# A SwiGLU kernel's prologue: x in two loads, first weight pieces in slices, transposed x evicted by slice

## The chip, the cores and the metric

One core of one Trainium2 chip. The metric is the device time of one execution in microseconds (us), 126.12 us for the kernel before (median of the first 4 runs). The profile's span, from the first to the last instruction, is 1.7 us shorter than the time of the same run (124.8 against 126.54). "TensorE's clock" below is the clock that the trace grants to the matrix engine: full rate or half.

In the profile's lines PE is TensorE, the matrix engine (PEld its weight loads), DVE is VectorE, ACT is ScalarE, and SPq and ACTq are the queues on which SyncE and ScalarE issue loads. A timeline line gives the start, the length, the engine with its source line and operation, and in brackets the idle time before it and what ended it. A line of stretches gives the stretch, its length, the busy time and count of PE, PEld, DVE, ACT and POOL, then the granted clock, the DMA engines' busy share and GB/s. A semaphore is a counter on which an engine waits; each load here raises one by 16 increments.

## The reference

```python
def reference(x, w_gate, w_up, w_down):      # x: 1 x 2048 x 512, weights 512 x 1376 and 1376 x 512, bf16
    g = silu(x @ w_gate)
    u = x @ w_up
    return (g * u) @ w_down
```

## The kernel before

x is worked on in four chunks of 512 rows. The matmuls contract over D = 512, which is four slices (dt) of 128, so x must be transposed. For chunks 1 to 3 a DMA transposes it while chunk 0 is computed. For chunk 0 TensorE does it in the prologue, by 128 x 128 transposes against an identity matrix, and VectorE and ScalarE copy the results (they "evict" them) from PSUM, where TensorE writes, to SBUF, where it reads its operands. After that TensorE runs groups of four matmuls (one per slice) for gate and up, and 44 for the down projection of a chunk.

The prologue, as the change and the argument touch it:

```python
WARM_PLAN = [(5, 512), (0, 256), (2, 256), (1, 256), (2, 256)]   # dummies (count, columns)
# SyncE's queue                      # ScalarE's queue
dma_x(sp, 0)                         dma_x(act, 1)      # 128 rows of x each, 128 KB
dma_x(sp, 2)                         dma_x(act, 3)
dma_w(sp, wg, ..., 0)                # w_gate, columns of groups 0 to 3, all four slices: 512 KB
dma_w(sp, wu, ..., 0)                # w_up, the same
dma_w(sp, wg, ..., 1); dma_w(sp, wu, ..., 1)        # the rest, 864 KB each
...                                  # w_down
# TensorE
for st in range(4):                  # row blocks
    dummy(*WARM_PLAN[st])            # matmuls on zeros, to bring the clock up
    transposes(st)                   # 4 transposes, after row block st has landed
dummy(*WARM_PLAN[4])
wait for all four evictions of xT    # VectorE, ScalarE, VectorE, ScalarE, one row block each
for ft in ...:                       # gate group: waits once for the whole weight piece
    for dt in range(4): matmul(pg, wg[:, dt, ft], xT[:, dt, chunk])
```

## Time and profile before

| what | value | how to read it |
|---|---|---|
| time | 126.12 us, 125.95 to 126.54 in 4 runs | more runs later fell in two clusters, see the result |
| first useful matmul | 8.15 us | nothing before it is part of the result |
| transposed x complete | 6.81 us | end of ScalarE's last copy |
| first gate piece landed | 8.01 us | 16th of its 16 semaphore increments |
| one useful matmul of 512 columns | 0.216 us start to start | no gaps after 8.15 |

Everything after 8.15 is a closed row of matmuls and a tail of 2.5 us. The prediction below shows the lines.

### The profile page before, as it was taken

What the parts mean: (1) busy time and instruction counts of PE and PEld (TensorE: products, weight loads), DVE (VectorE), ACT (ScalarE), POOL (GpSimd) and SP (SyncE); (2) the same over time, 40 slices, a digit from 0 to 9 for tenths busy, and PEclk for the clock granted to TensorE, in tenths of its full rate; (3) what the DMA queues carried; (4) which work ended last, traced back from release to release, by engine and by line L of the source; (5) the groups of instructions that cost most, each with busy time, mean ns of one, the idle gap of its engine ahead of it and who ended that gap; (6) DMA issues with size and microseconds to landing.
All of it is one profiled execution on the core that took longest, in us unless ns stands there. A gap on an engine that the chain in (4) does not pass through costs nothing.

```text
span 124.8 us, 1408 instructions
## 1 busy us (share of the span) xinstructions
PE 119.1 (95%) x565; PEld 56.2 (45%) x565; DVE 31.6 (25%) x48; ACT 38.3 (31%) x64; POOL 0.7 (1%) x6
## 2 busy tenths in 40 slices
PE   6849999999999999999999999999999999999992
PEld 1614444454444444454444444454444444454471
DVE  0204334440003344431002443332002433342001
ACT  4223333231133332331125323331114233321330
POOL 2000000000000000000000000000000000000000
PEclk9999999999999999999999999999999999999999
DMA  3899929890211000000211000000121000000112
GB/s 90 253 364 399 351 65 91 195 222 1 84 42 42 0 0 5 0 0 0 78 48 42 3 5 0 3 0 0 42 84 42 0 5 0 0 0 0 42 66 60
DMA packets 12822, 8.51 MB, mean 68 GB/s; under 512 B 6704, under 2 KB 12816, under 8 KB 12816
## 3 DMA queue, kind: packets, MB, share of 16 engines
q1 hardware_dynamic: 12528, 8.16, 24.4%
q10 hardware_dynamic: 288, 0.26, 0.7%
q8 instruction: 4, 0.07, 0.3%
q14 instruction: 2, 0.02, 0.0%
HBM read 4.75 MB, written 2.10 MB: 55 GB/s over the span
## 4 chain that ended last, share of the span: by engine, by line
PE 92%; DMA 5%; SPq 1%; DVE 0%; issue 0%
PE psum L226 31%; PE psum L240 30%; PE psum L281 29%; DMA wg<-in_w_gate_dram 5%; PE psum L269 2%; SPq L111 1%; DVE o_sb L351 0%
## 5 line engine op out<-in xcount | busy, mean ns | idle before, releaser
L338 DVE TENSOR_TENSOR hT<-sg,psum 128x512 bf16<-128x512 f32 (+1 forms) x44 | 30.2, 687 | 77.2 <-PE psum L240 77.2
L226 PE MATMUL psum<-xT,wg 128*128 128x512 bf16 (+1 forms) x176 | 45.0, 379 | 1.8 <-DMA wg<-in_w_gate_dram 1.8
L240 PE MATMUL psum<-xT,wu 128*128 128x512 bf16 (+1 forms) x176 | 45.0, 379 | 0.0
L305 ACT ACTIVATE sg<-psum 128x512 f32<-128x512 f32 (+1 forms) x44 | 26.3, 597 | 48.4 <-PE psum L226 48.4
L281 PE MATMUL psum<-wd,hT 128*128 128x512 bf16 (+1 forms) x165 | 36.3, 379 | 0.0
L226 PEld LDWEIGHTS psum<-xT,wg 128*128 128x128 bf16 (+1 forms) x176 | 17.5, 100 | 22.3 <-issue 2.0
L240 PEld LDWEIGHTS psum<-xT,wu 128*128 128x128 bf16 (+1 forms) x176 | 17.6, 100 | 20.4
L281 PEld LDWEIGHTS psum<-wd,hT 128*128 128x128 bf16 (+1 forms) x165 | 16.1, 98 | 19.4
L313 ACT ACTIVATE o_sb<-psum 128x512 bf16<-128x512 f32 x15 | 9.0, 597 | 30.2 <-PE psum L281 30.2
L191 PE MATMUL psum<-zeros 128*128 128x512 bf16 (+1 forms) x10 | 3.7, 494 | 1.1 <-DVE zeros L326 1.1
L351 DVE CAST o_sb<-psum 128x256 bf16<-128x256 f32 x1 | 0.4, 425 | 8.9 <-PE psum L269 8.9
L269 PE MATMUL psum<-wd,hT 128*128 128x256 bf16 (+1 forms) x22 | 2.6, 272 | 0.0
L201 PE MATMUL psum<-ident,x_nat 128*128 128x128 bf16 x16 | 2.2, 297 | 0.4 <-DMA x_nat<-in_x_dram 0.4
L201 PEld LDWEIGHTS psum<-ident,x_nat 128*128 128x128 bf16 x16 | 1.8, 140 | 1.5 <-issue 1.3
L269 PEld LDWEIGHTS psum<-wd,hT 128*128 128x128 bf16 (+1 forms) x22 | 2.1, 97 | 0.5
L191 PEld LDWEIGHTS psum<-zeros 128*128 128x128 bf16 x10 | 1.1, 132 | 1.9 <-DVE zeros L326 1.1
L330 DVE COPY xT<-psum 128x512 bf16<-128x512 bf16 x2 | 0.8, 425 | 4.3 <-PE psum L201 4.3
L296 ACT ACTIVATE xT<-psum 128x512 bf16<-128x512 bf16 x2 | 1.2, 598 | 2.4 <-PE psum L201 2.4
L292 ACT ACT_TABLE_LOAD x1 | 1.3, 1283 | 1.7 <-PEq L365 1.7
L311 ACT ACTIVATE o_sb<-psum 128x256 bf16<-128x256 f32 x1 | 0.4, 384 | 0.6 <-PE psum L269 0.6
L326 DVE MEMSET zeros<- 128x64 uint32 x1 | 0.1, 112 | 0.9 <-PEq L365 0.9
L174 POOL TENSOR_SCALAR_AFFINE_SELECT ident<-ones 128x128 bf16<-128x128 bf16 x1 | 0.3, 292 | 0.1
(6 smaller groups left out, 0.8 us busy)
## 6 DMA issues: line engine op xcount, KB each, us to landing
out_dram<-o_sb SPq DMA_DIRECT2D x15, 128.0 KB, 1.7
wd<-in_w_down_dram SPq DMA_DIRECT2D x2, 512.0 KB, 10.9
wg<-in_w_gate_dram SPq DMA_DIRECT2D x1, 864.0 KB, 9.0
wu<-in_w_up_dram SPq DMA_DIRECT2D x1, 864.0 KB, 10.8
wg<-in_w_gate_dram SPq DMA_DIRECT2D x1, 512.0 KB, 6.3
wu<-in_w_up_dram SPq DMA_DIRECT2D x1, 512.0 KB, 7.3
x_nat<-in_x_dram SPq DMA_DIRECT2D x2, 128.0 KB, 2.9
x_nat<-in_x_dram ACTq DMA_DIRECT2D x2, 128.0 KB, 3.1
```

The source lines that it names most:

```text
L111: eng.dma_start(x_nat[:, st, :], x_view[:, st, :]).then_inc(s_x[st], 16)
L191: pe.matmul(pg[:, 0, 0:width], zeros[:, :], zeros[:, 0:1].broadcast_to([P, width]), start=True, stop=True,)
L201: ins = pe.transpose(dstv[:, dt, :], x_nat[:, st, dt * P:(dt + 1) * P], ident[:])
L226: ins = pe.matmul(pg[0:fs, b, :], wg[:, dt, ft * P:ft * P + fs], xT[:, dt, sc * NS:(sc + 1) * NS], start=(dt == 0), stop=(dt == DT - 1),)
L240: ins = pe.matmul(pu[0:fs, b, :], wu[:, dt, ft * P:ft * P + fs], xT[:, dt, sc * NS:(sc + 1) * NS], start=(dt == 0), stop=(dt == DT - 1),)
L269: ins = pe.matmul(psum[:, bank, half * h:(half + 1) * h], hT[0:fs, ft, j * P:(j + 1) * P], wd[0:fs, ft, half * h:(half + 1) * h], start=(f ...
L281: ins = pe.matmul(po[:, j % 2, :], hT[0:fs, ft, j * P:(j + 1) * P], wd[0:fs, ft, :], start=(ft == 0), stop=(ft == FT - 1),)
L292: act.activation(scr[:, 0:1], zeros[:, 0:1], ACT_FN.Silu)
L296: act.activation(tp_dst(st), tp_src(st), ACT_FN.Copy).then_inc(s_xTa, 1)
L305: act.activation(sg[0:fs, b, :], pg[0:fs, b, :], ACT_FN.Silu).then_inc(s_sg, 1)
L313: act.activation(o_sb[:, j, :], po[:, j % 2, :], ACT_FN.Copy).then_inc(s_oe, 1)
L338: dve.tensor_tensor(hT[0:fs, ft, sc * NS:(sc + 1) * NS], sg[0:fs, b, :], pu[0:fs, b, :], ALU.mult).then_inc(s_h, 1)
```

## The change

Its intent is to let the first useful matmul start earlier: fewer and larger x loads, so that the weights are issued earlier; first weight pieces cut by slice, so that TensorE can begin with the first slice; and x evicted by slice for the same reason.

```diff
-WARM_PLAN = [(5, 512), (0, 256), (2, 256), (1, 256), (2, 256)]
+N_WARM0 = 6      # dummies of 512 columns, then 4 of 128, then none
+N_FILL0 = 4
+XT_EVAC_ENG = ["v", "a", "v", "v"]
...
+        def dma_x(eng, h):           # 256 rows, two neighbouring rows (2 KB) a partition
+            src = x2[h * HB:(h + 1) * HB, :].rearrange("(p q) d -> p q d", q=2)
+            eng.dma_start(x_nat[:, 2 * h:2 * h + 2, :], src).then_inc(s_x[h], 16)
+        def dma_wa(eng, dst, view, sems, dt):     # one slice, 128 KB
+            eng.dma_start(dst[:, dt, 0:FA * P], view[:, dt, 0:FA * P]).then_inc(sems[dt], 16)
...
             dma_x(sp, 0)
-            dma_x(sp, 2)
-            dma_w(sp, wg, wg_view, s_wg, 0)
-            dma_w(sp, wu, wu_view, s_wu, 0)
+            dma_wa(sp, wg, wg_view, s_wga, 0)
+            dma_wa(sp, wg, wg_view, s_wga, 2)
+            for dt in range(DT):
+                dma_wa(sp, wu, wu_view, s_wua, dt)
...
             dma_x(act, 1)
-            dma_x(act, 3)
+            dma_wa(act, wg, wg_view, s_wga, 1)
+            dma_wa(act, wg, wg_view, s_wga, 3)
...
+            dummy(N_WARM0, 512)
+            dummy(N_FILL0, 128)
+            transposes(0)            # 8 transposes; bank dt gets slice dt
+            transposes(1)            # 8 more; slice dt is signalled after its last one
...
                     for dt in range(DT):
+                        wait_xT(sc, dt)                   # slice dt of x
+                        if ft < FA:
+                            wait_once(s_wga[dt], 16)      # slice dt of the weights
                         ins = pe.matmul(...)
```

Cut: the stores of the first chunk, which become two of 256 KB because the rows of a half now lie in pairs, and the waits of the up groups, which change as the gate's do.

More of the change, by code (lines that the diff above doesn't have):

```diff
@@ L9 @@
 FP32 = mybir.dt.float32
-WARM_PLAN = [(5, 512), (0, 256), (2, 256), (1, 256), (2, 256)]
+N_WARM0 = 6
+N_FILL0 = 4
+N_WARM_MID = 0
+N_WARM_END = 0
+XT_EVAC_ENG = ["v", "a", "v", "v"]
 def bass_standalone__swiglu_ffn__prompt_kernel(
@@ L33, in bass_standalone__swiglu_ffn__prompt_kernel @@
     STC = NS // P
-    NPAIR = SC * FT
-    assert D % P == 0 and S % NS == 0 and D <= 512
+    assert D % P == 0 and S % NS == 0 and D <= 512 and STC == 4
     def fsz(ft):
         return min(P, F - ft * P)
-    w_pieces = [(0, 4), (4, 11)]
+    FA = 4
     wd_pieces = [(0, 4), (4, 8), (8, 11)]
@@ L52, in bass_standalone__swiglu_ffn__prompt_kernel @@
         wd_ndma.append((1 if nfull > 0 else 0) + (1 if (b > F // P and F % P) else 0))
-    tp_bank = [4, 5, 6, 7]
-    tp_eng = ["v", "a", "v", "a"]
-    tp_idx = [0, 0, 1, 1]
     with contextlib.ExitStack() as es:
@@ L83, in bass_standalone__swiglu_ffn__prompt_kernel @@
         psum_bf = psum[:, :, :].bitcast(BF16)
+        TP_BANK0 = 4
         s_zero = sem("s_zero")
@@ L98, in bass_standalone__swiglu_ffn__prompt_kernel @@
         s_od = sem("s_od")
-        s_x = [sem("s_x%d" % k) for k in range(STC)]
+        s_x = [sem("s_x%d" % k) for k in range(2)]
         s_xt = [sem("s_xt%d" % c) for c in range(SC)]
-        s_wg = [sem("s_wg%d" % k) for k in range(len(w_pieces))]
-        s_wu = [sem("s_wu%d" % k) for k in range(len(w_pieces))]
+        s_wga = [sem("s_wga%d" % dt) for dt in range(DT)]
+        s_wua = [sem("s_wua%d" % dt) for dt in range(DT)]
+        s_wgb = sem("s_wgb")
+        s_wub = sem("s_wub")
         s_wd = [sem("s_wd%d" % k) for k in range(len(wd_pieces))]
-        x_view = x2.rearrange("(st p) d -> p st d", p=P)
         wg_view = w_gate.rearrange("(dt p) f -> p dt f", p=P)
@@ L108, in bass_standalone__swiglu_ffn__prompt_kernel, with dma_wb @@
         out_view = out2.rearrange("(st p) d -> p st d", p=P)
-        def dma_x(eng, st):
-            eng.dma_start(x_nat[:, st, :], x_view[:, st, :]).then_inc(s_x[st], 16)
-        def dma_w(eng, dst, view, sems, k):
-            a, b = w_pieces[k]
-            fa, fb = a * P, min(b * P, F)
-            eng.dma_start(dst[:, :, fa:fb], view[:, :, fa:fb]).then_inc(sems[k], 16)
+        HB = NS // 2
+        def dma_x(eng, h):
[3 more added lines that the diff above has]
+            eng.dma_start(dst[:, dt, 0:FA * P], view[:, dt, 0:FA * P]).then_inc(sems[dt], 16)
+        def dma_wb(eng, dst, view, s_):
+            eng.dma_start(dst[:, :, FA * P:F], view[:, :, FA * P:F]).then_inc(s_, 16)
         def dma_wd(eng, k):
@@ L127, in dma_wd, with tp_src, tp_dst @@
                 eng.dma_start(wd[0:r, ft, :], w_down[ft * P:F, :]).then_inc(s_wd[k], 16)
-        def tp_src(st):
-            return psum_bf[:, tp_bank[st], 0:DT * P].rearrange("p (dt s) -> p dt s", dt=DT)
-        def tp_dst(st):
-            return xT[:, :, st * P:(st + 1) * P]
+        def tp_src(dt):
+            return psum_bf[:, TP_BANK0 + dt, 0:NS]
+        def tp_dst(dt):
+            return xT[:, dt, 0:NS]
+        stores = []
+        for h in range(2):
+            dst = out2[h * HB:(h + 1) * HB, :].rearrange("(p q) d -> p q d", q=2)
+            stores.append((2 * h, 2, dst))
+        for j in range(STC, ST):
+            stores.append((j, 1, out_view[:, j, :]))
         @block.sync
@@ L137, in _ @@
             dma_x(sp, 0)
-            dma_x(sp, 2)
-            dma_w(sp, wg, wg_view, s_wg, 0)
-            dma_w(sp, wu, wu_view, s_wu, 0)
-            dma_w(sp, wg, wg_view, s_wg, 1)
-            dma_w(sp, wu, wu_view, s_wu, 1)
-            dma_wd(sp, 0)
-            dma_wd(sp, 1)
-            dma_wd(sp, 2)
-            for k in range(STC):
-                sp.wait_ge(s_x[k], 16)
-            for k in range(len(w_pieces)):
-                sp.wait_ge(s_wg[k], 16)
-                sp.wait_ge(s_wu[k], 16)
+            dma_wa(sp, wg, wg_view, s_wga, 0)
+            dma_wa(sp, wg, wg_view, s_wga, 2)
+            for dt in range(DT):
+                dma_wa(sp, wu, wu_view, s_wua, dt)
+            dma_wb(sp, wg, wg_view, s_wgb)
+            dma_wb(sp, wu, wu_view, s_wub)
+            for k in range(len(wd_pieces)):
+                dma_wd(sp, k)
+            for k in range(2):
+                sp.wait_ge(s_x[k], 16)
+            for dt in range(DT):
+                sp.wait_ge(s_wga[dt], 16)
+                sp.wait_ge(s_wua[dt], 16)
+            sp.wait_ge(s_wgb, 16)
+            sp.wait_ge(s_wub, 16)
             for k in range(len(wd_pieces)):
@@ L158, in _ @@
                 sp.wait_ge(s_xt[c], 16)
-            for j in range(ST):
-                sp.wait_ge(s_oe, j + 1)
-                if j == ST - 1:
+            nst = 0
+            for (j0, n, dst) in stores:
+                jl = j0 + n - 1
+                sp.wait_ge(s_oe, jl + 1)
+                if jl == ST - 1:
                     h = D // 2
-                    sp.dma_start(out_view[:, j, 0:h], o_sb[:, j, 0:h]).then_inc(s_od, 16)
+                    sp.dma_start(dst[:, 0:h], o_sb[:, jl, 0:h]).then_inc(s_od, 16)
                     sp.wait_ge(s_oev, 1)
-                    sp.dma_start(out_view[:, j, h:D], o_sb[:, j, h:D]).then_inc(s_od, 16)
-                else:
-                    sp.dma_start(out_view[:, j, :], o_sb[:, j, :]).then_inc(s_od, 16)
-            sp.wait_ge(s_od, 16 * (ST + 1))
+                    sp.dma_start(dst[:, h:D], o_sb[:, jl, h:D]).then_inc(s_od, 16)
+                    nst += 2
+                elif n == 1:
+                    sp.dma_start(dst, o_sb[:, j0, :]).then_inc(s_od, 16)
+                    nst += 1
+                else:
+                    sp.dma_start(dst, o_sb[:, j0:j0 + n, :]).then_inc(s_od, 16)
+                    nst += 1
+            sp.wait_ge(s_od, 16 * nst)
         @block.gpsimd
@@ L194, in dummy, with transposes, wait_xT @@
                     )
-            def transposes(st):
-                wait_once(s_x[st], 16)
-                dstv = tp_src(st)
-                ins = None
+            def transposes(h):
+                wait_once(s_x[h], 16)
                 for dt in range(DT):
-                    ins = pe.transpose(dstv[:, dt, :], x_nat[:, st, dt * P:(dt + 1) * P], ident[:])
-                ins.then_inc(s_tp, 1)
-            wait_once(s_zero, 1)
-            for st in range(STC):
-                dummy(*WARM_PLAN[st])
-                if st == 0:
-                    wait_once(s_ident, 1)
-                transposes(st)
-            dummy(*WARM_PLAN[STC])
-            for sc in range(SC):
+                    ins = None
+                    for q in (2 * h, 2 * h + 1):
+                        ins = pe.transpose(
+                            psum_bf[:, TP_BANK0 + dt, q * P:(q + 1) * P],
+                            x_nat[:, q, dt * P:(dt + 1) * P],
+                            ident[:],
+                        )
+                    if h == 1:
+                        ins.then_inc(s_tp, 1)
+            wait_once(s_zero, 1)
+            dummy(N_WARM0, 512)
+            dummy(N_FILL0, 128)
+            wait_once(s_ident, 1)
+            transposes(0)
+            dummy(N_WARM_MID, 128)
+            transposes(1)
+            dummy(N_WARM_END, 128)
+            def wait_xT(sc, dt):
                 if sc == 0:
-                    for st in range(STC):
-                        wait_once(s_xTv if tp_eng[st] == "v" else s_xTa, tp_idx[st] + 1)
+                    e = XT_EVAC_ENG[dt]
+                    n = sum(1 for d2 in range(dt + 1) if XT_EVAC_ENG[d2] == e)
+                    wait_once(s_xTv if e == "v" else s_xTa, n)
                 else:
                     wait_once(s_xt[sc], 16)
+            for sc in range(SC):
                 def gate_group(ft):
@@ L223, in gate_group @@
                         wait_once(s_sg, i - 1)
-                    wait_once(s_wg[piece_of(ft, w_pieces)], 16)
+                    if ft >= FA:
+                        wait_once(s_wgb, 16)
                     for dt in range(DT):
+                        wait_xT(sc, dt)
+                        if ft < FA:
+                            wait_once(s_wga[dt], 16)
                         ins = pe.matmul(
@@ L237, in up_group @@
                         wait_once(s_h, i - 1)
-                    wait_once(s_wu[piece_of(ft, w_pieces)], 16)
+                    if ft >= FA:
+                        wait_once(s_wub, 16)
                     for dt in range(DT):
+                        wait_xT(sc, dt)
+                        if ft < FA:
+                            wait_once(s_wua[dt], 16)
                         ins = pe.matmul(
@@ L289, in _, with evac_xT @@
             dma_x(act, 1)
-            dma_x(act, 3)
+            dma_wa(act, wg, wg_view, s_wga, 1)
+            dma_wa(act, wg, wg_view, s_wga, 3)
             act.wait_ge(s_zero, 1)
             act.activation(scr[:, 0:1], zeros[:, 0:1], ACT_FN.Silu)
-            def evac_xT(st):
-                act.wait_ge(s_tp, st + 1)
-                act.activation(tp_dst(st), tp_src(st), ACT_FN.Copy).then_inc(s_xTa, 1)
+            def evac_xT(dt):
+                act.wait_ge(s_tp, dt + 1)
+                act.activation(tp_dst(dt), tp_src(dt), ACT_FN.Copy).then_inc(s_xTa, 1)
             def silu(i):
@@ L313, in evac_out @@
                     act.activation(o_sb[:, j, :], po[:, j % 2, :], ACT_FN.Copy).then_inc(s_oe, 1)
-            for st in range(STC):
-                if tp_eng[st] == "a":
-                    evac_xT(st)
+            for dt in range(DT):
+                if XT_EVAC_ENG[dt] == "a":
+                    evac_xT(dt)
             for sc in range(SC):
@@ L326, in _, with evac_xT @@
             dve.memset(zeros[:], 0.0).then_inc(s_zero, 1)
-            def evac_xT(st):
-                dve.wait_ge(s_tp, st + 1)
-                dve.tensor_copy(tp_dst(st), tp_src(st)).then_inc(s_xTv, 1)
+            def evac_xT(dt):
+                dve.wait_ge(s_tp, dt + 1)
+                dve.tensor_copy(tp_dst(dt), tp_src(dt)).then_inc(s_xTv, 1)
             def mul(i):
@@ L340, in mul @@
                 ).then_inc(s_h, 1)
-            for st in range(STC):
-                if tp_eng[st] == "v":
-                    evac_xT(st)
+            for dt in range(DT):
+                if XT_EVAC_ENG[dt] == "v":
+                    evac_xT(dt)
             for sc in range(SC):
```

## The prediction

> **What bounds the kernel now.** I read four views in this order: the page's busy table and its chain that ended last, to see which engine carries the end; the chain in order of time over the first 13 us, to see where that engine starts; the timeline of the same stretch, to see what it waited for and what was already ready; and busy time with DMA rate in chosen stretches, to see how the loads flow.
>
> The page, busy table and chain by engine and line:
>
> ```profile
> PE 119.1 (95%) x565; PEld 56.2 (45%) x565; DVE 31.6 (25%) x48; ACT 38.3 (31%) x64; POOL 0.7 (1%) x6
> ...
> PE 92%; DMA 5%; SPq 1%; DVE 0%; issue 0%
> PE psum L226 31%; PE psum L240 30%; PE psum L281 29%; DMA wg<-in_w_gate_dram 5%; PE psum L269 2%; SPq L111 1%; DVE o_sb L351 0%
> ```
>
> TensorE is 92% of the chain; what is left is nearly all one DMA, the first piece of w_gate (5% of 124.8 us, 6.3 us). So the kernel is a block of matmuls with a prologue ahead of it, and this change touches only the prologue.
>
> The chain in order of time, start and length in us:
>
> ```profile
> 1.25 0.42 SPq L111
> 1.67 0.05 issue
> 1.72 6.29 DMA wg<-in_w_gate_dram
> 8.01 0.14 issue
> 8.15 1.89 PE psum L226 x8
> 10.04 1.73 PE psum L240 x8
> 11.76 0.86 PE psum L226 x4
> ```
>
> The reader is to see two things. The first useful matmul starts at 8.15. After it a group of four takes 0.86, 0.216 us a matmul, without a gap: 517 matmuls of 512 columns at 0.216 us are 111.7 us, the 22 of 256 columns in the last tile take 2.42 us in this same chain, and 8.15 + 111.7 + 2.4 = 122.3 of a span of 124.8. The last 2.5 us are the last eviction and store. All that a prologue can win is in the 8.15.
>
> The timeline, what was ready before 8.15:
>
> ```profile
> 3.79 1.01 PE L201 MATMUL psum<-ident,x_nat 128*128 128x128 bf16 x8 [0.42 <-DMA x_nat<-in_x_dram]
> 4.41 0.42 DVE L330 COPY xT<-psum 128x512 bf16<-128x512 bf16 x1 [3.41 <-PE psum L201]
> ...
> 6.21 0.60 ACT L296 ACTIVATE xT<-psum 128x512 bf16<-128x512 bf16 x1 [0.78 <-PE psum L201]
> 8.12 1.42 PEld L226 LDWEIGHTS psum<-xT,wg 128*128 128x128 bf16 x8 [2.01 <-issue]
> 8.15 1.89 PE L226 MATMUL psum<-xT,wg 128*128 128x512 bf16 x8 [1.75 <-DMA wg<-in_w_gate_dram]
> ```
>
> The transposed x is complete when ScalarE's last copy ends, 6.21 + 0.60 = 6.81. TensorE then idles 1.75 us in all until the 512 KB gate piece lands at 8.01. So two chains end near each other: x (load, transpose, evict) at 6.81, weights at 8.01.
>
> Busy time and DMA in stretches (last two columns: DMA share, GB/s):
>
> ```profile
> 2.50:3.50 1.00, 0.87 (x3) 0.00 (x0) 0.00 (x0) 0.71 (x2) 0.00 (x0) 1.00 1.02 356
> 3.50:6.50 3.00, 2.60 (x21) 2.15 (x21) 0.85 (x2) 0.89 (x2) 0.00 (x0) 1.00 0.86 240
> 6.50:8.00 1.50, 0.00 (x0) 0.00 (x0) 0.00 (x0) 0.31 (x1) 0.00 (x0) 1.00 1.04 346
> 8.00:12.00 4.00, 3.85 (x18) 1.78 (x19) 0.89 (x2) 1.19 (x2) 0.00 (x0) 1.00 1.06 402
> ```
>
> The loads run at 356 GB/s while x comes in, fall to 240 between 3.5 and 6.5, when the gate piece is fetched, and recover. In the packets of the trace I find the reason for the dip: most 1 KB packets take 46 ns, but between 3.6 and 6.0 nine take from 0.4 to 1.1 us. The 16 semaphore increments of the gate piece show what it costs: eight of them stand at 5.60 to 5.83, twelve by 6.60, the last four at 7.14, 7.25, 7.89 and 8.01. The same tail is in the first w_up piece (first increment 7.33, last 9.51). The x loads have no such tail (0.5 us from the first to the last, all four landed at 3.65 to 4.44).
>
> **What the Trainium skill says.** (1) "DMA: Bandwidth & Descriptors", section "Why a DMA increments its semaphore by 16 and not by 1": only the full 16 means that all the data has landed. The trace agrees: TensorE left at 8.15, after the 16th increment at 8.01, though half had come by 5.83. (2) Same page, "Issuing engines are not separate DMA queues": transfers issued from SyncE and ScalarE run on the same 16 engines, and a second issuer saves issue time only. So moving two gate pieces to ScalarE's queue adds no bandwidth; it saves one issue of 0.4 to 0.5 us. (3) "TensorE: Matmul & The Clock Gate", "Part 1: The HAM clock gate", says that matmuls run at half rate until some 3.4 us of sustained activity, and that the window is free-running. The trace agrees in kind: dummy matmuls of 512 columns start 0.427 us apart from 1.05 on, transposes start 0.107 us apart until about 5.8, then faster, and all useful matmuls run at 0.216.
>
> **The change part by part.**
>
> *x in two loads of 256 KB, 2 KB a partition, in place of four.* Removed: one issue on each queue. SyncE's first weight load starts at 1.25 instead of 1.72, and ScalarE's at the same time. Bytes are the same 0.52 MB. Four loads landed at 3.65, 3.85, 4.22 and 4.44; the two halves share the engines, so I expect both at 4.1 to 4.3. The first transposes then start at about 4.2, not 3.79. The dummies end just before: 1.05 + 6 x 0.427 + 4 x 0.107 = 4.04.
>
> *16 transposes without dummies between them, evicted by slice of D (dt) rather than by row block.* Cold, 16 x 0.107 = 1.71 us: 4.2 to 5.9. The signal for slice dt comes with its last transpose in the second half. In the trace before, VectorE's copy starts 0.35 us after its last transpose starts (4.06 to 4.41). So slice 0 (VectorE, 0.425 us) is ready near 6.0, slice 1 (ScalarE, 0.60) near 6.4, slice 2 (VectorE) near 6.45, and slice 3 (VectorE, after slice 2) at 6.45 + 0.43 = 6.9. The end of this chain is therefore where it was, 6.81. What changes is that TensorE needs only slice 0 for its first matmul.
>
> *Gate and up first pieces in four loads of 128 KB each, one semaphore each.* The bytes ahead of the last gate slice are the same (x and 0.52 MB of w_gate, 1.05 MB), at rates that I take to be the same; the queue is fed about 0.5 us earlier but the engines are busy with x then. The slow packets I expect again. I put the last gate slice at 7.6 (0.4 before the old 8.01, between the twelfth increment of 6.6 and the old end), and the last up slice at 9.2 (old 9.51).
>
> *Stores: the first four in two of 256 KB.* They lie tens of us ahead of the end, and the last store is unchanged: 0.
>
> *Sum.* The shift is set where TensorE last waits. If x alone bound, the fourth matmul of the first group (slice 3) starts at about 7.0 where it started at 8.15 + 3 x 0.216 = 8.80: a gain of 1.8. With the last gate slice at 7.6 it starts at 7.7: gain 1.1. The fourth matmul of the first up group started at 8.15 + 11 x 0.216 = 10.52; with the last up slice at 9.2 it can start at 9.3: gain 1.2 at most. The large w_up piece landed at 14.06 and its first user started at 15.91, so 1.8 of shift fits. The smallest counts: 1.1 us, and 126.12 - 1.1 = 125.0.
>
> **The rivals.** (a) *Slow packets gone or hidden:* the x chain binds and the gain is 1.8, time 124.3. For it: the wait becomes one per slice, so early slices hide behind later ones. Against it: a slow DMA engine is late for every slice queued behind the slow packet. (b) *The weights keep their landing:* the last gate slice at 8.0 still, only the first three matmuls of the group move ahead of it, gain 0.65 (8.80 against 8.15), and the up slices at 9.5 leave 0.9: time 125.5. For it: same bytes, same engines, some 100 more small semaphore writes. (c) *The clock:* with TensorE starting useful work by 6.1 rather than 8.15, the end of the cold phase (about 5.8 in this trace) may fall among useful matmuls. A cold 512-column matmul costs 0.427, 0.21 more than a warm one; 2 us of it takes back 1.0 us. Time 125.3 to 126. Before, the wait for weights hid any late warming. Nothing in one trace tells how the phase falls. (d) *Issue:* SyncE has eight issues ahead of the large w_up piece instead of five, some 1.2 us later (3.29 to about 4.5), but its queue has a backlog until 7.3, when the first up piece begins to finish: no cost.
>
> **Range and chances.** A gain of 2% is 2.5 us, more than the 1.8 that the x chain leaves even with all weights there, so faster by over 2% needs the x chain itself to shorten by 0.7 us: 4%. A loss of 2% would need the prologue to grow by 2.5 us; only a long cold phase together with later weights would do it: 1%. Four runs of before span 0.6 us. The range 124.2 to 125.9 holds rivals (a), (b) and most of (c).
>
> **What would show it.** Right: first useful matmul at 6.0 to 6.6, small gaps in the first two gate and up groups put down to weight DMAs, no gap after the first 14 us, last 2.5 us unchanged. Wrong: a first group released by VectorE's last copy with no DMA wait (rival a); gate matmuls at 0.427 us (rival c); a wait at the large w_up piece (my slack of 1.8 was too small); or x landing well before 4.0, which would lengthen the gain beyond 1.8.

## The result, and the profile after

The changed kernel is correct and takes 124.57 us (median of 11 runs, 124.07 to 124.91). Beside it, the kernel before gave 16 runs in two clusters: eight at 125.92 to 126.58 and eight at 127.73 to 128.33. The stated ratio, 0.984 (95% interval 0.980 to 0.988), is the mean time of the changed kernel's fast runs over that of the other's fast runs of the same rounds, so not quite the ratio of the medians; two runs at 127.7 and 127.8 still counted as fast. With all 16 runs of before counted, the slower cluster in full, its mean is 127.14 and the changed kernel is 2.1% faster. Against the lower cluster alone (mean 126.16) the changed kernel's mean of 124.47 is 1.68 us less, ratio 0.987. Below, "lower cluster" means the runs of before under 127.2 us, and a gain is the difference of means against the lower cluster of the same job.

The page after, busy table and chain, the lines that answer to the first fence of the prediction:

```profile
PE 119.5 (97%) x565; PEld 56.4 (46%) x565; DVE 32.0 (26%) x49; ACT 37.7 (31%) x63; POOL 0.7 (1%) x6
...
PE 94%; DMA 3%; DVE 0%; issue 0%
PE psum L259 31%; PE psum L277 31%; PE psum L319 29%; DMA x_nat<-in_x_dram 3%; PE psum L307 2%; PE psum L221 2%; DVE o_sb L390 0%
```

The weight DMA has gone from the chain. What stands ahead of the useful matmuls now is the x load (3%) and the transposes (L221, 2%).

The chain in order of time (start us, length us):

```profile
0.80 3.42 DMA x_nat<-in_x_dram
4.22 0.14 issue
4.36 1.86 PE psum L221 x16
6.22 2.18 PE psum L259 x8
8.40 1.73 PE psum L277 x8
10.12 0.86 PE psum L259 x4
```

From 4.36 on TensorE never stops: 16 transposes, then useful matmuls. The first eight of them take 2.18 us where eight at full rate take 1.73 (the next line). In the single records the first three start at 6.10, 6.50 and 6.93, so two are at about half rate; the trace's clock record grants the full rate from 6.94 on. (The page's row of granted clock does not show a half rate ahead of the first record: it reads 9 in the first slices, where dummies of 512 columns start 0.427 us apart. There the spacing of the matmuls is the witness.) The fourth starts at 7.15, where it started at 8.80 before: 1.65 us earlier. The span fell by 1.6 (124.8 to 123.2). In twelve of the fourteen traces of this case the span ends 116.00 to 116.03 us after the start of the fourth useful matmul (e2 116.10, e10 117.00), and the run's time is 117.73 to 117.77 us more than that start. So this one start carries the whole change, and a time less 117.75 gives an estimate of it for runs without a trace.

The timeline around the eviction:

```profile
4.36 1.86 PE L221 MATMUL psum<-ident,x_nat 128*128 128x128 bf16 x16
5.62 1.18 DVE L369 COPY xT<-psum 128x512 bf16<-128x512 bf16 x3 [4.62 <-PE psum L221]
5.83 0.60 ACT L335 ACTIVATE xT<-psum 128x512 bf16<-128x512 bf16 x1 [2.12 <-PE psum L221]
6.10 0.10 PEld L259 LDWEIGHTS psum<-xT,wg 128*128 128x128 bf16 x1
6.10 2.30 PE L259 MATMUL psum<-xT,wg 128*128 128x512 bf16 x8
```

The last copy still ends at 5.62 + 1.18 = 6.80, as before, but the first matmul no longer waits for it: it starts at 6.10, as soon as slice 0 is there.

Stretches (the last two columns are DMA share and GB/s):

```profile
2.50:3.50 1.00, 1.00 (x4) 0.30 (x2) 0.00 (x0) 0.99 (x1) 0.00 (x0) 1.00 1.02 397
3.50:6.50 3.00, 2.86 (x22) 2.12 (x21) 0.88 (x3) 0.80 (x2) 0.00 (x0) 1.00 1.07 323
6.50:8.00 1.50, 1.50 (x7) 0.65 (x7) 0.30 (x1) 0.43 (x1) 0.00 (x0) 1.00 1.01 366
```

Between 3.5 and 6.5 the loads now run at 323 GB/s instead of 240. TensorE is busy for all of the 1.5 us from 6.5 to 8.0, in which it did nothing before.

### The profile page after: what moved, and what is told of

Same layout as the page of the kernel before. It is cut to its first block, busy times and chain, and to the rows that moved or that the text cites. A ratio compares the mean times of both kernels' runs of the same rounds, so it can differ in the third digit from the quotient of the medians.

```text
span 123.2 us, 1414 instructions
## 1 busy us (share of the span) xinstructions
PE 119.5 (97%) x565; PEld 56.4 (46%) x565; DVE 32.0 (26%) x49; ACT 37.7 (31%) x63; POOL 0.7 (1%) x6
## 4 chain that ended last, share of the span: by engine, by line
PE 94%; DMA 3%; DVE 0%; issue 0%
PE psum L259 31%; PE psum L277 31%; PE psum L319 29%; DMA x_nat<-in_x_dram 3%; PE psum L307 2%; PE psum L221 2%; DVE o_sb L390 0%
## 5 line engine op out<-in xcount | busy, mean ns | idle before, releaser
L211 PE MATMUL psum<-zeros 128*128 128x512 bf16 (+1 forms) x10 | 3.2, 504 | 1.1 <-DVE zeros L365 1.1
L221 PE MATMUL psum<-ident,x_nat 128*128 128x128 bf16 x16 | 1.9, 311 | 0.1
L221 PEld LDWEIGHTS psum<-ident,x_nat 128*128 128x128 bf16 x16 | 1.6, 146 | 0.4 <-issue 0.4
L335 ACT ACTIVATE xT<-psum 128x512 bf16<-128x512 bf16 x1 | 0.6, 597 | 2.1 <-PE psum L221 2.1
```

Of the source, the lines that this page charges most:

```text
L211: pe.matmul(pg[:, 0, 0:width], zeros[:, :], zeros[:, 0:1].broadcast_to([P, width]), start=True, stop=True,)
L221: ins = pe.transpose(psum_bf[:, TP_BANK0 + dt, q * P:(q + 1) * P], x_nat[:, q, dt * P:(dt + 1) * P], ident[:],)
L335: act.activation(tp_dst(dt), tp_src(dt), ACT_FN.Copy).then_inc(s_xTa, 1)
```

## The experiments

Twelve kernels, in three jobs, each job with its own runs of the kernel before on the same chip. Two questions: which part of the change gives the 1.68 us, and what the upper cluster of the kernel before is.

The loads' finish in each trace, read from the semaphore increments (us; "12th" and "16th" are the time by which every piece or slice had that many of its 16 increments) and from the packet records (packets of 1 or 1.7 KB that took 0.4 us or longer between 3.4 and 8 us; the normal is 0.046 and 0.072):

| kernel of the trace | gate 12th | gate 16th | up 16th | slow packets |
|---|---|---|---|---|
| before | 6.60 | 8.01 | 9.51 | 9 |
| e1 (before again) | 5.83 | 7.52 | 8.87 | 6 |
| e4 | 6.78 | 7.47 | 8.99 | 13 |
| e10 | 6.61 | 7.79 | 9.21 | 14 |
| e2 | 7.19 | 7.50 | 9.61 | 14 |
| after | 6.20 | 6.25 | 7.47 | 5 |
| e5 (after again) | 5.99 | 6.16 | 7.40 | 7 |
| e6 | 6.14 | 6.62 | 7.69 | 5 |
| e7 | 5.96 | 6.10 | 7.34 | 4 |
| e9 | 5.93 | 6.27 | 7.42 | 3 |
| e11 | 6.14 | 6.38 | 7.65 | 5 |
| e3 | 5.74 | 6.35 | 7.84 | 0 |
| e8 | 5.94 | 6.81 | 8.56 | 13 |
| e12 | 6.14 | 7.39 | 8.68 | 3 |

### e1: the kernel before again

No edit.

> The kernel before, unchanged, against itself. Its timed runs fell in two clusters, 125.9 to 126.6 and 127.7 to 128.3 us; the changed kernel's lie all within 124.07 to 124.91. Theory A (clock): in the slow cluster TensorE falls back to half rate in its 1.75 us of idleness and runs the first useful matmuls at 0.427 us; then both clusters show again and the slow runs have a granted clock below 1.000. Theory B (loads): in the slow cluster the first gate piece lands some 2 us later than 8.0; then the clock is 1.000 in all and a slow trace shows the first useful matmul near 10. The ratio should be 1.00 in either.

Measured: 14 runs, eight at 125.38 to 126.41, four at 127.66 to 127.98 and two at 129.43 and 129.64, which I cannot explain; ratio 1.002. The clusters are real and belong to the kernel. The profiled run (126.05) was of the lower one: its first useful matmul stood at 7.65, its clock was 1.000.

The record decides it without a trace, because it holds the mean granted clock of every run in the three jobs. Of the 98 runs of before in them, all 72 of the lower cluster read 0.998 to 1.000, and 23 of the 26 at 127.2 us and over read 0.986 or 0.987; of the six slow runs of e1 itself, the three at 127.87 to 127.98 read 0.986. Half rate for 3.413 us (the stretch that e10's trace shows) in a span of 126.3 gives 1 - 1.71 / 126.3 = 0.986. So nearly all of the upper cluster is theory A, the clock. Those runs lie 1.7 to 2.0 us above the lower cluster of their job; 3.413 us at half rate explain at most 1.7 of that. The six others (127.66 to 129.64, clock 1.000) stay open: a reading of 1.000 does not exclude a cold start, since the half rate ahead of the first clock record is not counted, and the traces of e1, e2, e3 and e12 hold no such record at all.

### e2: the weight slices alone

```diff
-            dma_w(sp, wg, wg_view, s_wg, 0)
-            dma_w(sp, wu, wu_view, s_wu, 0)
+            dma_wa(sp, wg, wg_view, s_wga, 0); dma_wa(sp, wg, wg_view, s_wga, 2)
+            for dt in range(DT): dma_wa(sp, wu, wu_view, s_wua, dt)
...  # slices 1 and 3 of w_gate behind the x loads on ScalarE's queue; one wait per slice
```

> The kernel before with the per-slice weight loads and their waits alone (x loads, dummies, transposes and evictions as before). If the earlier weights are the gain (theory W): last gate slice by 6.6, first useful matmul at 6.85 when ScalarE's last copy ends, gain over before 1.2 to 1.3 us, ratio 0.990. If the eviction by slice is the gain (theory E): the gate slices still land at 8.0 because the slow packets stay, first useful matmul before 8 but the fourth near 8.1, gain 0.6, ratio 0.995.

Measured: 125.34 us median of 22 runs, none in the upper cluster. Mean 125.30, 0.68 us below the lower cluster of the job (125.98); ratio 0.9945. The chain of this kernel:

```profile
6.36 0.61 ACT xT L315
6.97 0.25 issue
7.21 1.89 PE psum L240 x8
9.10 1.81 PE psum L257 x8
```

The first useful matmul now waits for the last copy of x (ScalarE's, 6.97), not for the gate: the weights' wait was removed and the x chain stood just behind it. The profiled run (125.71) was the slowest of the 22, and in it the gate bound as well: the slow packets stayed (14), the third slice came at 7.50, and the third matmul started at 7.64, where the first one's start put it too. In the median run (125.34) the x chain alone would give the time (an estimate: last copy at 6.81 to 6.86, as in the traces of before and e1, fourth matmul 0.75 to 0.90 later, as in those of e7 and e2, and 117.75 more: 125.3 to 125.5). In the profiled run the up slices came late enough to stretch the second line of eight from 1.73 to 1.81. The time fits theory E's number, and the first useful matmul (7.21) lies between the two theories.

### e3: the changed kernel with whole weight pieces

```diff
-            dma_wa(sp, wg, wg_view, s_wga, 0) ... (8 slices on two queues)
+            sp.dma_start(wg[:, :, 0:FA * P], wg_view[:, :, 0:FA * P]).then_inc(s_wga[0], 16)
+            sp.dma_start(wu[:, :, 0:FA * P], wu_view[:, :, 0:FA * P]).then_inc(s_wua[0], 16)
```

> The changed kernel with the first gate and up piece as one load of 512 KB each on SyncE's queue, all else changed. Theory W (cutting the weights brings them forward): the gate piece lands at 7.5 to 8.0 with four of its 16 increments late, first useful matmul at 7.7 to 8.1, most of the gain gone (ratio to before 0.997 or more). Theory E (merged x loads and eviction by slice do it): gate piece lands by 6.3, first useful matmul near 6.4, ratio about 0.987.

Measured: 125.11 us median of 12 runs (one slow one at 126.84), mean 125.22, gain 0.76, or 0.91 without the slow run; ratio 0.993. The profiled run was the fastest of them (124.9) and had no slow packet at all; its gate piece landed at 6.35:

```profile
6.01 0.43 DVE xT L364
6.45 0.04 issue
6.48 1.89 PE psum L256 x8
8.37 1.73 PE psum L274 x8
```

The chain puts the start at 6.48 down to VectorE's second copy, which ended at 6.44, but that is not what the code waits for: the first matmul needs the first slice of x, which VectorE's first copy had ready at 6.01, and the whole gate piece, whose 16th increment came at 6.35. It started 0.13 us after that, as it did after the 16th increment in before (0.14), e1, e4 and e10. So even in its fastest run the whole piece set the start, though it landed where theory E put it. The median lies between the theories. With e2, the two halves of the change give 0.68 and 0.76 to 0.91 alone and, in the two jobs with the whole, 1.68 and 1.47 together: about the sum. Each half alone runs into the wait that the other removes.

What in the second half earns its part was not isolated. Eviction by slice (e7) and the merged x loads (e12) are each not told apart from nothing below. What remains is that no dummies stand between the transposes any more. The trace of e10, which drops them from the kernel before, supports it: its last copy of x ended at 5.73, not 6.81, in part because the clock came at 4.31. No run changes this alone.

### e4: the kernel before with its gap filled

```diff
-WARM_PLAN = [(5, 512), (0, 256), (2, 256), (1, 256), (2, 256)]
+WARM_PLAN = [(5, 512), (0, 256), (2, 256), (1, 256), (12, 256)]
```

> The kernel before with 12 instead of 2 dummies of 256 columns after the last transpose, which fill TensorE's wait for the gate piece (12 x 0.107 = 1.3 us warm, 2.6 cold). Theory A (clock lost in the idle wait makes the slow cluster): only the fast cluster is left, at 125.9 to 126.8 us. Theory B (late loads): both clusters stay, 2 us apart.

Measured: 22 runs at 125.48 to 126.71, none in the upper cluster, where before had 17 of its 57 runs of the same job there. The mean, 126.34, is 0.36 above the lower cluster. Ten dummies on zeros, which compute nothing, take the upper cluster away. In its trace the loads were as slow as ever (gate 7.47, 13 slow packets), so theory B falls.

### e10: the kernel before without its later dummies

```diff
-WARM_PLAN = [(5, 512), (0, 256), (2, 256), (1, 256), (2, 256)]
+WARM_PLAN = [(5, 512), (0, 256), (0, 256), (0, 256), (0, 256)]
```

> The kernel before with its first five dummies alone, none between or after the transposes, so TensorE works less and idles from about 5.5 to 8. Theory A (the slow cluster of before at 127.6 to 128.3 is a clock that is not released, or lost again, ahead of the useful matmuls): the slow cluster takes more of the runs than its share of about a third, possibly all, and a trace of a slow run shows useful matmuls 0.427 us apart after 7.5. Theory B (loads): same clusters in the same shares as before, all useful matmuls at 0.216.

Measured: four runs, all in the upper cluster or above it (127.9 and 127.98 at a clock of 0.986, 128.6 and 128.93 at 1.000), ratio 1.018. The trace is of the run at 127.9. TensorE's timeline, then busy time in three stretches (the third column from the right is the granted clock, then DMA share and GB/s):

```profile
3.75 1.31 PE L201 MATMUL psum<-ident,x_nat 128*128 128x128 bf16 x16 [0.38 <-DMA x_nat<-in_x_dram]
7.92 3.46 PE L226 MATMUL psum<-xT,wg 128*128 128x512 bf16 x8 [2.87 <-DMA wg<-in_w_gate_dram]
11.22 1.89 PE L240 MATMUL psum<-xT,wu 128*128 128x512 bf16 x8
```

```profile
4.40:7.70 3.30, 0.66 (x12) 0.48 (x9) 0.82 (x2) 1.08 (x2) 0.00 (x0) 1.00 0.91 268
7.80:11.10 3.30, 3.18 (x8) 1.17 (x9) 0.00 (x0) 0.60 (x1) 0.00 (x0) 0.50 1.06 405
11.20:14.60 3.40, 3.40 (x17) 1.57 (x16) 1.37 (x2) 1.19 (x2) 0.00 (x0) 1.00 1.08 365
```

This is the lost clock itself. Eight matmuls take 3.46 us where the next eight take 1.89. The clock record reads: full rate from 4.31 to 7.73, half from 7.73 to 11.14, full again after; both pieces last 3.413 us. In the first stretch TensorE worked 0.66 us of 3.3, and then lost the full rate just as the gate piece landed (7.79). From 7.92 to 11.14 at half rate costs half of 3.2, 1.6 us. That the upper cluster of the unchanged kernel is the same thing was not caught in a trace of it. The evidence is that 23 of its 26 runs have the same clock, 0.986 or 0.987 (see e1), that it lies at the same times and that it goes when the gap is filled. When the gap is widened no run is left in the lower cluster; two of the four have that clock, the other two stay open.

### e5: the changed kernel again, as control

No edit.

> The changed kernel unchanged, as the control of this set. Expected 1.65 us below the fast cluster of before (125.4 to 126.6), no run in a slow cluster, last gate slice near 6.3, fourth useful matmul near 7.15.

Measured: six runs at 124.26 to 124.95, mean 124.53, gain 1.47 on a lower cluster of 126.00 (nine runs; five others in the upper one). Fourth useful matmul at 6.68 (in the trace of after it was 7.15; there the full rate came at 6.94, here at 6.25), gate slices in at 6.16.

### e6: x in descriptors of 1 KB

```diff
-.rearrange("(p q) d -> p q d", q=2)
+.rearrange("(q p) d -> p q d", q=2)      # load and first stores
```

> The changed kernel with each half of x read as 256 descriptors of 1 KB (two row blocks apart) instead of 128 of 2 KB; still two loads, same bytes. In four traces with four 1 KB x loads the gate piece landed at 7.47 to 8.01, in two with merged x at 6.25 and 6.35. Theory M1 (it is the 2 KB descriptors that free the engines): slow packets come back, last gate slice at 7.3 to 8, time 0.4 to 1.0 us above the control. Theory M2 (it is the number of loads, so the earlier issue of the weights, or chance): last gate slice by 6.6, time within 0.2 us of the control.

Measured: mean 124.53, as the control; last gate slice at 6.62, 5 slow packets. M1 falls: the 2 KB runs are worth nothing here.

### e7: eviction by row block

```diff
-            return psum_bf[:, TP_BANK0 + dt, 0:NS]                # bank dt, slice dt
+            return psum_bf[:, TP_BANK0 + q, 0:NS].rearrange(...)  # bank q, row block q, all slices
...
-                    wait for slice dt of xT
+                    wait_once(s_xTv, 2); wait_once(s_xTa, 2)      # all four
```

> The changed kernel with the transposed x evicted by row block (VectorE, ScalarE, VectorE, ScalarE) and the first matmul waiting for all four, as in the kernel before. Theory E (eviction by slice is part of the gain): the last copy ends near 6.85, the fourth useful matmul starts at 7.55 instead of 7.15, time 0.4 us above the control. Theory W (only the weights gained): TensorE's first three matmuls are cold and bought nothing, time within 0.1 us of the control.

Measured: mean 124.63, 0.10 above the control; the standard deviations are 0.13 and 0.21 over six runs each (95% interval of the difference -0.15 to 0.36), so this is not told apart from nothing, and theory E's 0.4 is out. A likely reason, argued and not shown, is in the two chains: in the changed kernel the matmuls that start early do so at half rate (7.15 for the fourth), and the row-block copies, shared two and two between VectorE and ScalarE, begin as soon as the first row block is transposed. In this trace the last copy was done at 6.17, before the first useful matmul at 6.27, when TensorE had its full rate (granted from 4.73); the fourth stood at 6.91. The clock came 1.5 to 2.2 us earlier in this trace than in the two of the changed kernel, so the traces do not compare the two evictions alone.

### e8: all gate slices on SyncE's queue

```diff
+            for dt in range(DT): dma_wa(sp, wg, wg_view, s_wga, dt)
-            dma_wa(act, wg, wg_view, s_wga, 1); dma_wa(act, wg, wg_view, s_wga, 3)
```

> The changed kernel with all four gate slices on SyncE's queue. If the second queue matters, the gate slices start later: two more issues of 0.46 us before the up slices; up slices land 0.5 later, gate slices the same to 0.3 later, time 0 to 0.3 us above the control. If it does not (the 16 engines are the limit): within 0.1 us.

Measured: nine runs, mean 124.90, 0.37 above the control (124.53; 95% interval 0.00 to 0.75), spread 124.02 to 125.47. Gate slices in at 6.81, up slices at 8.56, 13 slow packets. The later issue explains it in size, but the slow packets are also more than in the control, and one trace of each does not separate the two.

### e9: the changed kernel without dummies

```diff
-N_WARM0 = 6
-N_FILL0 = 4
+N_WARM0 = 0
+N_FILL0 = 0
```

> The changed kernel without any dummy matmuls: TensorE starts with the transposes near 4.1. The clock was released at 4.2 to 6.9 us in the traces so far, with work from 1.05 on. If it takes sustained work to release it, it now comes at 7.5 to 11, so 1.5 to 4 us of useful matmuls run at 0.427 us, and half of that is lost: 0.8 to 2 us above the changed kernel (125.3 to 126.5). If the dummies are idle ballast, the time is within 0.2 us of it.

Measured: 20 runs, 124.89 to 126.54, mean 125.71, gain 0.42 on its lower cluster (126.14) instead of 1.47 to 1.68. So the dummies are worth 1.05 to 1.26 us. The profiled run was one of the fast ones (124.98): TensorE started at 4.26 and had the full rate at 7.19, with three useful matmuls ahead of it. My range for the release, 7.5 to 11, began too late. The spread of 1.65 us is what one window of 3.413 us at half rate would make if its place against the kernel's start were arbitrary (3.413 / 2 = 1.71); that it is arbitrary is an inference from the spread. The ten traces with a clock record, of kernels with and without dummies, fit it: the full rate came at 4.2 to 7.2 us.

### e11: half of x evicted during the transposes, a try for a better version

```diff
-                            psum_bf[:, TP_BANK0 + dt, q * P:(q + 1) * P],
+                            psum_bf[:, (2 + dt // 2) if h == 0 else TP_BANK0 + dt, ...],
...  # first half: two copies of two slices each (VectorE, ScalarE); second half: four copies of 256 columns
```

> A try for a version that beats both. The changed kernel with the first half of x evicted while the second half is transposed (its transposes go to two other banks), so that after the last transposes copies of 256 columns remain instead of 512. VectorE's three last copies should take 0.25 us instead of 0.42, first useful matmul 0.2 earlier, fourth 0.3 earlier. If the x chain binds in the changed kernel, 0.2 us faster than it (124.25); if the gate slices (last at 6.0 to 6.3) or the cold clock bind, no change within 0.1.

Measured: 124.33 us median of six runs, mean 124.40, gain 1.73, against 1.47 and 1.68 of the changed kernel in its two jobs: not told apart from it. Its chain and what the first gate group did:

```profile
4.26 0.73 PE psum L226 x8
4.99 0.02 issue
5.01 0.88 ACT xT L341 x2
5.89 0.05 issue
5.94 1.81 PE psum L265 x7
```

The first useful matmul came at 5.52, as hoped, but the second waited for ScalarE's pair of copies until 5.94 and the fourth for the last gate slice (16th increment at 6.38; start 6.51). The x chain was shortened and the wait went to ScalarE and the weights. (That a first version of this edit was refused by the check before the chip, and the first half moved to other PSUM banks for it, is not in the record.)

### e12: the changed kernel with x in four loads

```diff
-            dma_x(sp, 0)                                 # 256 KB
+            dma_x(sp, 0); dma_x(sp, 2)                   # 128 KB each
-            dma_x(act, 1)
+            dma_x(act, 1); dma_x(act, 3)
...  # the load function, its semaphores and the transposes' waits for four loads; the rows stay in pairs
```

> The changed kernel with x in four loads of 128 KB again, all else as changed. If merging the x loads brings the weights forward: each queue's weights are issued 0.46 us later, slow packets are as many as in the two traces with four x loads and slices or two-byte-for-byte equal pieces (6 to 14 over 0.4 us, against 4 to 7 in the changed kernel), last gate slice at 6.6 to 7.5, time 0.3 to 0.9 us above the changed kernel. If merging is worth nothing: within 0.1 us, and the last gate slice stays by 6.4.

Measured: six runs, four at 124.37 to 124.55 and two at 125.31 and 125.40; mean 124.75, gain 1.39. The trace is of the run at 125.31. In it 15 of the 16 increments of the last gate slice were in by 6.30 and the 16th came at 7.39: one engine was late, in every slice, and TensorE's first useful matmul stood at 6.61, 0.14 after the first slice's 16th increment (6.47). In four of the other five runs, which have no trace, the time is the control's; the fifth (125.40) is as late as this one. Merging the x loads is therefore worth nothing in most runs, and what it may do is to spare a late engine in some; six runs do not settle that.

## Why the prediction was right or wrong

The time, 124.57, lies in the range (124.2 to 125.9), and the gain over the lower cluster (1.3%) stays under the 2% that the prediction gave 4%. But the path that it named as the binding one, the last gate slice, was not: the x chain bound, with two matmuls at half rate behind it, nearly as rival (a) had it, and the range held that. The number 125.0 was also nearer than its own timeline by luck: the shift of 1.1 was read from the trace of a run of 126.54 and taken off the median of 126.12, while a fourth matmul at 7.7 means 7.7 + 117.75 = 125.45. Step by step:

- **What bounds it, and the ceiling.** Right. All of the change lies ahead of the first useful matmuls; the tail is unchanged, and the span fell by as much (1.6) as the fourth useful matmul moved (1.65).
- **The x chain.** Right, and to a tenth: x halves at 4.1 to 4.3 predicted, 4.22 and 4.39 measured; last copy at 6.9, measured 6.80. In the profiled run the fourth matmul started at 7.15 and not 7.0, because the prediction let the first matmuls run as soon as their slices were ready, and two ran at half rate. That was rival (c) in small. The median run, 124.57, puts that start near 6.8 (an estimate, less 117.75), so the ceiling held.
- **The last gate slice at 7.6.** This is the term that was mis-sized. It came at 6.25, and in all six traces with sliced weights on two queues and two x loads, e6's 1 KB variant included, at 6.10 to 6.62. The last up slice came at 7.47, not 9.2. So the smallest of the three limits was not 1.1 but the x chain's, and rival (a) is what happened. I had carried the slow packets over unchanged.
- **Why the late increments went.** Not settled. It is not the slicing alone (e2: 7.50, 14 slow packets), not the 2 KB descriptors (e6: 6.62, 5). The one queue in e8 and the four loads in e12 had late engines again (6.81 and 7.39), but e3, on one queue with whole pieces, had none in its only trace. The count of slow packets does not tell it alone: e12 has 3, and its last engine was 1.1 us late. The 12th increment moves little, 5.7 to 6.8 in all but one trace; it is the last four that differ.
- **Eviction by slice.** Overrated. I wrote that this is what changes in the x chain; e7 shows it to be worth 0.10, not told apart from nothing.
- **The large w_up piece.** Right: it was in at 12.44, before its user at 14.28 in the timeline, and no wait shows.
- **What I did not see.** That the idle wait for the gate piece also put the clock at risk. In all jobs together 34 of the 114 runs of before were at 127.2 us and over. Of the changed kernel's 17 runs none was. I had the half-rate phase as a danger for the changed kernel alone; it is the kernel before that paid for it, some 2 us in about a quarter of its runs (23 of the 98 whose clock is on record).

## What to carry to other kernels

When two chains end close to each other ahead of the first useful matmul, cutting one gains only the distance to the other; here each half alone gave 0.7 to 0.9 us and both about 1.5 to 1.7. A wait in which the matrix engine idles can cost more than its length, because the clock can be taken back during it; dummies that fill the wait, or a prologue without it, remove a slow cluster of runs that a single trace will not show. Run a kernel often enough to see whether its times fall in clusters before crediting a change with their mean, and read each run's granted clock: here it told the cause of a cluster of which no trace was caught.

## What the Trainium skill lacked or had wrong

- "TensorE: Matmul & The Clock Gate", "Part 1: The HAM clock gate": the window of 3413 ns agrees (e10: full rate for 3.413 us, half rate for 3.413 us). But the section "HAM oscillation — how this bites in real kernels" gives as the rule that idle gaps over some 3.4 us are to be avoided; in e10 a gap of 2.87 us was enough (the clock fell at 7.73, 2.7 us into it), with TensorE busy 0.66 us of 3.3.
- The same page calls the release a matter of some 3.4 us sustained work; in e9 the full rate was granted at 7.19 after 2.9 us of work (from 4.26), and in the ten traces with a clock record it came 2.9 to 5.9 us after the first matmul (in after at 6.94, with dummies and transposes from 1.05 on).
- The same page says that the ramp penalty is under 1% of a typical span; e9, which loses 1.05 to 1.26 us (0.8 to 1.0%), does not contradict it. The figure does not cover a clock that is lost again: the upper-cluster runs of before at a clock of 0.986 or 0.987 are 2.0 us above the lower cluster (128.00 against 125.98 in the largest job), 1.6%, for a single wait.
- "DMA: Bandwidth & Descriptors", "Issuing engines are not separate DMA queues", says that a second issuer saves only issue time, usually small; here the slices on one queue cost 0.37 us (e8 against e5, interval 0.00 to 0.75), which the 0.46 us of one issue would cover. Nothing here contradicts it.
- No page tells why some of these loads get a few packets of 1 KB that take 0.4 to 1.4 us (0 to 14 slow packets in a trace) where others with the same bytes get none, so that a piece's last increments come up to 1.7 us after its 12th (e1).
